# Small products and transposes in four column tiles: a two-layer attention and feed-forward kernel on one core

## The chip, the core and the metric

The kernel runs on one core of a Trainium2 chip. A core has five engines that work side by side and meet at semaphores: TensorE (matrix products, written to PSUM), VectorE, ScalarE, GpSimd, and SyncE, whose queue starts most transfers (SP in the profile). The metric is the device time of the program in microseconds; each kernel's time is the median of several runs. A profile is one execution taken by the hardware profiler; its span runs from the first to the last instruction.

TensorE computes `out = lhsT.T @ rhs`: a weight load puts `lhsT` into the array (PEld in the profile), a matmul streams `rhs` through it (PE). The array can be used in one piece, in four row tiles (four products with up to 32 rows of contraction each, side by side) or in four column tiles (four products with 32 output rows each, side by side). The profile shows this in the form: `128*128` is a whole product, `128*32` one of four column tiles, `32*128` or `16*128` a row tile.

## What is computed

Four layers alternate over x of 2048 x 512 in bf16: attention with a memory (A), feed-forward (B), A, B, each on a layer norm and added to x.

```
def A(x):   # 32 heads of 16, four segments of 512 rows
    q, k, v = heads(x @ wq), heads(x @ wk), heads(x @ wv)
    phi = lambda t: where(t > 0, t + 1, exp(t))
    M, z = 0, 0
    for s in range(4):
        a_dot = causal_softmax(q[s] @ k[s].T * scale) @ v[s]
        a_mem = (phi(q[s]) @ M) / (phi(q[s]) @ z + 1e-6)
        out[s] = g * a_mem + (1 - g) * a_dot
        M = M + phi(k[s]).T @ v[s]
        z = z + sum(phi(k[s]))
    return out @ wo
def B(x):
    return (gelu(x @ w_gate) * (x @ w_up)) @ w_down
```

In segment 0 the memory is empty, so the memory products run in segments 1 to 3, and the update of M in segments 0 to 2, in both attention layers.

## The kernel before

Everything lies in SBUF: x as 16 tiles of 128 x 512 (`x_sb`) and all weights. The two attention layers have four segments each, so that there are eight attention steps k = 0 to 7 (`Att`) and eight feed-forward steps (`Ffn`), one per segment and layer; step k of `Ffn` follows step k of `Att`, and step k + 4 of `Att` follows step k of `Ffn`. Work of several steps is interleaved.

The order of all instructions is made by a planner that runs in Python when the program is built. `Clocks` keeps an estimate of TensorE's time (`ck.pe`) and of each other engine's, with a cost for each operation; `Item` is a piece of TensorE work with a due time, a condition under which it is ready, its operations and what follows when they are done. The loop at the end of the kernel takes, in this order: a score step when a score buffer is free, the next operation of the opened item, a new item that is ready and has the earliest due time, or, when nothing of that is to be had and scores remain, one product of `warm` with itself whose result nobody reads. Each engine works through its instructions in the order so made; the planner's times decide that order only, and semaphores keep the data right.

TensorE's work, by the lines of the profile:

- Line 395, in `product`: all dense products (q, k, v, the output projection wo, gate, up, down), each 128 x 512 with a contraction of 128 per call, issued as four column tiles of 32 output rows. The unread products of `warm` in the loop are also made here.
- Line 800: scores, in row tiles, two heads to a score buffer `st` of two PSUM banks. ScalarE exponentiates them (line 829) into `pt`, GpSimd masks the diagonal blocks (line 820).
- Line 848: the flush, probabilities times v, in column tiles: 16 matmuls, four for each of four key blocks, with 512, 384, 256 and 128 columns. VectorE transposes the result back (line 860), divides and adds.
- Line 645, `den_mm`: phi(q) times z, 16 products of 128 x 8 for each attention step with a memory. Line 665, `num`: phi(q) times M, 16 products of 128 x 128 a step, four to an item. Line 716, `upd_item`: phi(k).T times v, 16 products of 128 x 128 a step, accumulated in one bank. All three are whole products.
- Line 486, `turn_item`: transposes of the normed rows `xn` into `xnT`. Most norms are transposed by a transfer on SP's queue (line 359). For three feed-forward steps, 0, 1 and 7 (`BY_PE`), TensorE does it, four 128 x 128 transposes for each of the four row tiles, as whole operations with a bf16 result in PSUM. Ahead of each four stand two unread whole products of 128 x 256 (line 484, `FILL = 2`), and the item counts as ready that much earlier. VectorE or ScalarE evicts the result (lines 385 and 386, in `evict`), whichever the planner finds free.

`ck.tiling(mode)` tells the planner's clock of a change of tiling and adds `SWITCH` to it; `whole(fn)` wraps an operation with `ck.tiling("whole")`. It emits nothing by itself. `ALWAYS = True` makes `product` take the column tiles in every case.

Of the kernel before, what the change touches and what calls it, by code (L numbers as in the profile page):

```python
# [14 lines left out]
BF16 = mybir.dt.bfloat16  # L15
I32 = mybir.dt.int32

P = 128
D = 512
H = 32  # L20
DH = 16
NSEG = 4
NK = 2 * NSEG
L = 512
NT = 16
KT = D // P
FF = 1792
FT = FF // P
TPS = L // P
# [20 lines left out]
EXP_SLACK, E_SLACK, PHI_SLACK, GELU_SLACK = -1.0, 3.0, 3.0, -1.0  # L50
ACT_EVICT, FIRST_EVICT = 0.5, 1.0
XN_BUFS = 3
FILL = 2
KB_DVE = 1
KB_SLACK = 4.0
HALF_STEPS = 1
MARGIN = 1.0
MEM_SLACK = 1.0
ALWAYS = True


class Engine:
# [157 lines left out]
def kernel(  # L220
# [14 lines left out]
    nc = tc.nc  # L235
# [9 lines left out]
    ck = Clocks()  # L245
# [30 lines left out]
    for n, (sb, w) in enumerate(((wg_sb, B_w_gate), (wu_sb, B_w_up))):  # L276
        for kt in range(KT):
            for h in range(2):
                c = slice(FF * h // 2, FF * (h + 1) // 2)
                pieces.append((37.0 + 1.6 * (8 * n + 2 * kt + h), 224, lambda sb=sb, w=w, kt=kt, c=c: load(  # L280
                    sb[:, kt, c], w_view(w)[:, kt, c])))
    for h in range(7):
        r = slice(2 * h, 2 * h + 2)
# [4 lines left out]
    warm = cst.tile([P, P], BF16, name="warm")  # L288
    wide = warm[:].unsqueeze(1).to_broadcast([P, 4, P])
    nc.vector.memset(warm[:], 1.0)  # L290

    def bank_tile(i, shape, dtype=F32):
        return psp.tile(shape, dtype, tag=f"m{i}", bufs=1, name="m")
# [11 lines left out]
    ident = cst.tile([P, P], BF16, name="ident")  # L305
# [21 lines left out]
    def by_head(va):  # L327
        return va[:, :, 0:VW].rearrange("p t (h e) -> p t h e", e=DH + 1)
# [24 lines left out]
    def turn_later(t, slack, out, in_, landed, margin=0.0):  # L353

        def told(t2):
            t3 = max(t2 + 1.4 + margin, ck.dma + 1.2)
            ck.at(t3 - 0.2, lambda: landed(t3))

        ck.sp.post(t, slack, (1.3, lambda: nc.sync.dma_start_transpose(out=out(), in_=in_()), told))
# [16 lines left out]
    def evict(ps, dst, src, told, slack=NORMAL):  # L376

        taken = []

        def end(t):  # L380
            ps.read(t)
            told(t)

        first = FIRST_EVICT if ("scores", HALF_STEPS - 1) not in ev and HALF_STEPS else ACT_EVICT
        ck.dve.post(ck.made(), slack, (0.673, lambda: nc.vector.tensor_copy(out=dst(), in_=src()), end), taken=taken)  # L385
        ck.act.post(ck.made(), slack + first, (0.602, lambda: nc.scalar.activation(  # L386
            out=dst(), in_=src(), func=ACT.Copy), end), taken=taken)

    def product(out, lhsT, rhs, start=True, stop=True):

        if ck.mode == "columns" or ALWAYS:
            ck.tiling("columns")
            for c in range(4):
                r = slice(32 * c, 32 * c + 32)
                nc.tensor.matmul(out[r], lhsT=lhsT[:, r], rhs=rhs, start=start, stop=stop, tile_position=(0, 32 * c))  # L395
        else:
            ck.tiling("whole")
            nc.tensor.matmul(out, lhsT=lhsT, rhs=rhs, start=start, stop=stop)

    def whole(fn):  # L400
        return lambda: (ck.tiling("whole"), fn())

    def dense(ps, pairs):
        n = len(pairs)
# [6 lines left out]
    class Norm:  # L411
# [64 lines left out]
        def turn_item(self, j, xn, t, landed):  # L476

            ps = Psum()
            half = L // 2

            def turned():
                return ps()[:, 0:half].bitcast(BF16).rearrange("p (k t) -> p k t", t=P)

            ops = [(Clocks.MM[512] / 2, whole(lambda: nc.tensor.matmul(
                ps()[:, half:L], lhsT=warm[:], rhs=wide[:, 0:2, :], start=True, stop=True)))] * FILL
            ops += [(Clocks.MM[128], whole(lambda kt=kt: nc.tensor.transpose(
                turned()[:, kt, :], xn()[:, kt * P:(kt + 1) * P], ident[:]))) for kt in range(KT)]
            return Item(-0.5, lambda: t + Engine.LATENCY <= ck.pe + FILL * Clocks.MM[512] / 2, ops,
                        lambda: evict(ps, lambda: self.xnT[:, :, j * P:(j + 1) * P], turned, landed, URGENT),
                        kind="turn", ps=ps)  # L490

# [11 lines left out]
    items = []  # L503
# [5 lines left out]
    class Att:  # L509
# [126 lines left out]
        def mem_items(self):  # L636
            k = self.k

            def ready(*more):
                return ck.has(*[("phiq", k, b) for b in range(4)], ("mem", k - 1), *more)  # L640

            den = Psum((P, TPS, 4, 8))

            def den_mm(j, b):
                nc.tensor.matmul(den()[:, j, b, :], lhsT=self.phiq[:, b, j * P:(j + 1) * P],  # L645
                                 rhs=mem_state[k - 1][1][:, b, :], start=True, stop=True)

            def den_done():
                def add():
                    self.rdm = wrk.tile([P, TPS, 4, 8], F32, tag="rdm", bufs=1, name="rdm")  # L650
                    nc.vector.tensor_scalar(out=self.rdm[:], in0=den()[:], scalar1=EPS_MEM, scalar2=None, op0=ALU.add)

                ck.dve.post(ck.made(), NORMAL, (0.273, add, den.read),
                            (0.956, lambda: nc.vector.reciprocal(out=self.rdm[:], in_=self.rdm[:]),
                             lambda t: ev.update({("den", k): t})))

            items.append(Item(k + 0.01, lambda: ready() and (self.s == 1 or ("am", k - 1) in ev),
                              [(Clocks.SMALL, whole(lambda j=j, b=b: den_mm(j, b))) for j in range(TPS) for b in range(4)],
                              den_done, kind="mem", ps=den))

            def num(b):
                ps = Psum()

                def mm(j):
                    nc.tensor.matmul(ps()[:, j * P:(j + 1) * P], lhsT=self.phiq[:, b, j * P:(j + 1) * P],  # L665
                                     rhs=mem_state[k - 1][0][:, b, :], start=True, stop=True)

                def done():
                    self.n_num += 1
                    if self.n_num == 4:  # L670
                        ev["memn", k] = ck.pe

                    def scale():
                        self.am = seg.tile([P, TPS, P], BF16, tag=f"am{b % 2}", bufs=1, name="am")
                        nc.vector.tensor_tensor(
                            out=self.am[:].rearrange("p t (h e) -> p t h e", e=DH),
                            in0=ps()[:].rearrange("p (t h e) -> p t h e", h=8, e=DH),
                            in1=self.rdm[:, :, b, :].unsqueeze(3).to_broadcast([P, TPS, 8, DH]),
                            op=ALU.mult)

                    def told(t):
                        ps.read(t)
                        am = self.am
                        self.n_am += 1
                        if self.n_am == 4:
                            ev["am", k] = t
                        self.amT[b] = seg.tile([P, L], BF16, tag=f"amT{b}", bufs=1, name="amT")
                        turn_later(t, NORMAL, lambda: self.amT[b][:].rearrange("p (t q) -> p t q", q=P),
                                   lambda: am[:].rearrange("p t d -> p (t d)"),
                                   lambda t2: ck.at(t2 + 1.0, lambda: ev.update({("amT", k, b): t2 + 1.0})))  # L690

                    ck.dve.post(ck.made(), NORMAL, (0.683, scale, told))

                def go():
                    return (ready(("den", k)) and (b < 2 or ("amT", k, b - 2) in ev)
                            and (self.s == 1 or (("amT", k - 1, (b + 2) % 4 if b < 2 else b) in ev
                                                 and ("aT", k - 1, b) in ev)))

                return Item(k + 0.02 + 0.001 * b, go, [(Clocks.MM[128], whole(lambda j=j: mm(j))) for j in range(TPS)], done,
                            kind="mem", ps=ps)  # L700

            for b in range(4):
                items.append(num(b))

        def upd_item(self):
            k = self.k
            psm = Psum((P, 4, P))
            n_mm = 4 * TPS
# [4 lines left out]

            def m(c):
                j, b = divmod(c, 4)
                nc.tensor.matmul(psm()[:, b, :], lhsT=self.phik[:, j, b * P:(b + 1) * P],  # L716
                                 rhs=by_head(self.vaug)[:, j, 8 * b:8 * b + 8, 0:DH], start=(c == 0), stop=(c == n_mm - 1))

            def done():
                ev["upd", k] = ck.pe  # L720
# [22 lines left out]
                else:  # L743
# [5 lines left out]
                             (0.2, z, told)]  # L749
                ck.dve.chain(ck.made(), MEM_SLACK, *steps)  # L750

            items.append(Item(k + 0.45, ready, [(Clocks.MM[128], whole(lambda c=c: m(c))) for c in range(n_mm)],
                              done, kind="upd", ps=psm))


# [250 lines left out]
    mem_state = {}  # L1006
# [40 lines left out]
    ps = bank_tile(1, [P, L])  # L1047
# [4 lines left out]
    ps, half = bank_tile(2, [P, L]), L // 2  # L1052
# [5 lines left out]
    ps = bank_tile(3, [P, L])  # L1058
# [24 lines left out]
    opened, half = None, 0  # L1083
# [49 lines left out]
    while streams or items or opened or ck.busy():  # L1133
# [3 lines left out]
        if halves:  # L1137
            half = score(halves)
            continue
        if opened:  # L1140
            cost, fn = opened.ops.pop(0)
# [14 lines left out]
        if halves:  # L1156
            half = score(halves)
            continue
        if min(banks) <= ck.pe:

            if streams:
                ps = Psum()
# [37 lines left out]
```

## Time and profile before

| | us |
|---|---|
| three runs, median | 567.98 |
| lowest and highest | 567.58, 568.27 |
| profiled execution, its span | 566.8 |
| ScalarE's exponentials of scores (line 829), busy | 310.6 |
| den products (line 645), busy | 3.8 |
| num products (line 665), busy | 8.1 |
| upd products (line 716), busy | 7.4 |
| transposes (line 486), busy | 4.6 |
| unread products ahead of them (line 484), busy | 5.0 |

A group's row reads: line, engine, operation, output<-inputs, form, count | busy time of the group, mean length of one in ns | idle time of the engine ahead of it, and who ended most of it. Matmul records overlap, since the next product starts while the one before runs out of the array: busy time and length of a record say less than the distance from one start to the next. A row of the timeline reads: start, length from the first start to the last end, engine, line, operation, tiles, form of the first, count of instructions merged.

### The profile page before, as it was taken

To read this page: it belongs to the slowest core of one execution; us is meant where nothing else is said; L and a number is where in the kernel's file an instruction comes from. 1 tells how busy PE (TensorE), PEld (TensorE's weight loads), DVE (VectorE), ACT (ScalarE), POOL (GpSimd) and SP (SyncE) were. 2 spreads that over 40 slices of the span, in tenths; PEclk is the share of its full clock that TensorE was granted. 3 is DMA by queue.
4 is the path that set the end of the run, shared out by engine and by line. 5 is a ranking of instruction groups with operands and counts; after the bars stand their busy time and mean duration, and the time that the engine had idled before them with its cause. 6 is when DMAs were issued, how large, how long until landed. Compare 5 with 4: busy or idle time off the path is not lost.

```text
span 566.8 us, 22572 instructions
## 1 busy us (share of the span) xinstructions
PE 557.4 (98%) x9966; PEld 259.0 (46%) x9966; DVE 460.5 (81%) x879; ACT 447.1 (79%) x512; POOL 271.1 (48%) x520
## 2 busy tenths in 40 slices
PE   8999999999999999999999999999999999999997
PEld 4433444444545444444444444444444444445554
DVE  5977989989999789878988989889688876787061
ACT  3899989988999779987889879988899776860600
POOL 2599854455542458435861557525664354310000
PEclk9999999999999999999999999999999999999999
DMA  7346613600330016200210124001320003100001
GB/s 223 41 104 196 132 20 41 159 13 16 44 60 1 3 39 78 31 12 2 54 26 3 30 43 72 12 3 30 87 39 3 3 12 86 21 2 30 12 3 39
DMA packets 64354, 25.85 MB, mean 46 GB/s; under 512 B 54272, under 2 KB 64256, under 8 KB 64256
## 3 DMA queue, kind: packets, MB, share of 16 engines
q1 hardware_dynamic: 64112, 24.40, 21.0%
q8 instruction: 78, 1.28, 1.0%
q14 instruction: 20, 0.16, 0.1%
q10 hardware_dynamic: 144, 0.01, 0.0%
HBM read 9.71 MB, written 2.10 MB: 21 GB/s over the span
## 4 chain that ended last, share of the span: by engine, by line
PE 86%; DVE 6%; ACT 5%; issue 2%; DMA 1%; POOL 0%; ACTq 0%
PE m L395 66%; PE st L800 9%; PE m L848 6%; ACT pt L829 2%; PE m L299 1%; PE m L716 1%; PE m L665 1%; ACT gel L1000 1%; DVE byq L860 1%; DMA phik<-e 1%; DVE aT L875 1%; DVE ab L868 1%; DVE st L424 0%; DVE q L385 0%; PE m L645 0%
## 5 line engine op out<-in xcount | busy, mean ns | idle before, releaser
L829 ACT ACTIVATE pt<-st 128x1024 bf16<-128x1024 f32 x320 | 310.6, 1028 | 55.5 <-PE st L800 48.4
L820 POOL TENSOR_SCALAR_AFFINE_SELECT pt<-pt 128x256 bf16<-128x256 bf16 (+1 forms) x448 | 204.9, 475 | 222.3 <-ACT pt L829 214.8
L395 PE MATMUL m<-xnT,wg_sb 128*32 128x512 bf16 x1792 | 108.3, 380 | 0.9 <-ACT xnT L386 0.7
L395 PE MATMUL m<-wd_sb,gel 128*32 128x512 bf16 x1792 | 105.6, 380 | 0.0
L395 PE MATMUL m<-xnT,wu_sb 128*32 128x512 bf16 x1792 | 102.8, 380 | 0.3 <-DVE vaug L385 0.3
L967 DVE TENSOR_TENSOR gel<-gel,m 128x512 bf16<-128x512 bf16 x112 | 74.4, 683 | 27.2 <-PE m L395 23.2
L395 PEld LDWEIGHTS <-wu_sb 128*32 128x32 bf16 x1792 | 47.9, 97 | 46.9 <-issue 4.5
L395 PEld LDWEIGHTS <-gel 128*32 128x32 bf16 x1792 | 46.0, 97 | 45.2 <-issue 5.1
L395 PEld LDWEIGHTS <-wg_sb 128*32 128x32 bf16 x1792 | 44.8, 96 | 46.0 <-issue 9.1
L914 DVE TENSOR_TENSOR x_sb<-x_sb,m 128x512 bf16<-128x512 bf16 x64 | 42.4, 675 | 23.3 <-PE m L395 23.0
L860 DVE STREAM_TRANSPOSE byq<-m 128x512 f32<-128x512 f32 x64 | 45.1, 706 | 14.3 <-PE m L848 13.9
L848 PE MATMUL m<-pt,vaug 128*32 128x512 bf16 (+3 forms) x1024 | 46.7, 301 | 0.1
L555 POOL TENSOR_SCALAR kB<-kf,maskB 128x512 bf16<-128x512 bf16 x28 | 44.4, 1586 | 4.4 <-DVE kf L385 3.1
L1000 ACT ACTIVATE gel<-gel 128x2048 bf16<-128x2048 bf16 (+1 forms) x28 | 45.2, 1685 | 0.1
L385 DVE CAST gel<-m 128x512 bf16<-128x512 f32 x56 | 37.8, 684 | 8.9 <-PE m L395 8.8
L424 DVE BATCH_NORM_STATS2 st<-x_sb 128x6 f32<-128x512 bf16 x60 | 40.7, 678 | 0.5
L800 PE MATMUL st<-q,kB 32*128 32x128 bf16 (+3 forms) x512 | 39.1, 300 | 0.8 <-ACT pt L829 0.7
L800 PE MATMUL st<-q,kf 16*128 16x384 bf16 (+3 forms) x512 | 39.1, 302 | 0.0
L848 PEld LDWEIGHTS <-vaug 128*32 128x32 bf16 x1024 | 25.3, 97 | 22.8 <-issue 2.8
L395 PE MATMUL m<-xnT,wq_sb 128*32 128x512 bf16 x496 | 33.9, 381 | 0.0
L395 PE MATMUL m<-xnT,wk_sb 128*32 128x512 bf16 x496 | 33.9, 381 | 0.0
L395 PE MATMUL m<-wo_sb,aT 128*32 128x512 bf16 x512 | 32.3, 380 | 0.9 <-DVE aT L878 0.8
(96 smaller groups left out, 563.7 us busy)
## 6 DMA issues: line engine op xcount, KB each, us to landing
out_dram<-x_sb SPq DMA_DIRECT2D x16, 128.0 KB, 1.7
wg_sb<-in_B_w_gate_dram SPq DMA_DIRECT2D x8, 224.0 KB, 4.7
wu_sb<-in_B_w_up_dram SPq DMA_DIRECT2D x8, 224.0 KB, 4.1
wd_sb<-in_B_w_down_dram SPq DMA_DIRECT2D x7, 256.0 KB, 4.9
x_sb<-in_A_x_dram SPq DMA_DIRECT2D x3, 512.0 KB, 6.1
xnT<-xn SPq DMA_TRANSPOSE x48, 2.6
x_sb<-in_A_x_dram SPq DMA_DIRECT2D x4, 128.0 KB, 2.8
wv_sb<-in_A_wv_dram SPq DMA_DIRECT2D x1, 512.0 KB, 7.0
```

What stands on the lines that cost most here:

```text
L385: ck.dve.post(ck.made(), slack, (0.673, lambda: nc.vector.tensor_copy(out=dst(), in_=src()), end), taken=taken)
L395: nc.tensor.matmul(out[r], lhsT=lhsT[:, r], rhs=rhs, start=start, stop=stop, tile_position=(0, 32 * c))
L424: nc.vector.bn_stats(out=self.st6[:, 0, :], in_=x_sb[:, self.tt0 + j, :])
L555: job.post(t, KB_SLACK if k else NORMAL, (cost, lambda: eng.tensor_scalar(out=self.kB[:, b, :], in0=self.kf[:, b, :], scalar1=maskB[:, 0:1 ...
L800: nc.tensor.matmul(sts[j // 2][:, j % 2, c0:c0 + N], lhsT=lhsT[rows, b, P * ki:P * ki + P], rhs=self.q[rows, b, P * ki:L], start=True, sto ...
L820: nc.gpsimd.affine_select(out=dv, in_=dv, pattern=[[0, w], [1, P]], compare_op=ALU.is_ge, fill=0.0, base=0, channel_multiplier=-1)
L829: ck.act.post(max(begun + 0.4, self.step_from), EXP_SLACK, (1.024, lambda st=st, pt=pt: nc.scalar.activation(out=pt[:], in_=st[:], func=AC ...
L848: nc.tensor.matmul(ps()[32 * j:32 * j + 32, P * ki:L], lhsT=self.vaug[:, ki, h * (DH + 1):h * (DH + 1) + 32], rhs=two[j // 2][:, j % 2, c0 ...
L860: nc.vector.transpose(out=self.byq[:, par, :, :].rearrange("p a c -> p (a c)"), in_=ps()[:])
L914: ck.dve.post(ck.made(), slack, (0.683, lambda: nc.vector.tensor_tensor(out=xt, in0=xt, in1=ps()[:], op=ALU.add), lambda t: (ps.read(t), t ...
L967: ck.dve.post(ck.made(), NORMAL, (0.683, lambda: nc.vector.tensor_tensor(out=g, in0=g, in1=ps()[:], op=ALU.mult), lambda t: (ps.read(t), e ...
L1000: return (0.205 + 0.427 * (f1 - f0), lambda: nc.scalar.activation(out=g, in_=g, func=ACT.Gelu_apprx_tanh), lambda t: ev.update({("gel", se ...
```

## The change

The memory products (den, num, upd) and the transposes of `turn_item` go through `product`, so that each is issued as four matmuls of 32 columns of weights in four column tiles. The transposes thereby become ordinary products with the identity, with an fp32 result that fills the whole PSUM bank instead of a bf16 result in its half; the evictions read fp32. The two unread products ahead of each four transposes go, and the item counts as ready when its xn is. `whole`, `FILL` and `ALWAYS` go. The planner's costs of the operations stay as they were per product. The four transposes of each row tile in the prologue (`first_turn`), and the prologue's products, stay whole.

```diff
-FILL = 2
-ALWAYS = True
@@ product
-        if ck.mode == "columns" or ALWAYS:
-            ck.tiling("columns")
-            for c in range(4):
-                r = slice(32 * c, 32 * c + 32)
-                nc.tensor.matmul(out[r], lhsT=lhsT[:, r], rhs=rhs, start=start, stop=stop, tile_position=(0, 32 * c))
-        else:
-            ck.tiling("whole")
-            nc.tensor.matmul(out, lhsT=lhsT, rhs=rhs, start=start, stop=stop)
-
-    def whole(fn):
-        return lambda: (ck.tiling("whole"), fn())
+        ck.tiling("columns")
+        for c in range(4):
+            r = slice(32 * c, 32 * c + 32)
+            nc.tensor.matmul(out[r], lhsT=lhsT[:, r], rhs=rhs, start=start, stop=stop, tile_position=(0, 32 * c))
@@ turn_item
-            half = L // 2
-                return ps()[:, 0:half].bitcast(BF16).rearrange("p (k t) -> p k t", t=P)
-            ops = [(Clocks.MM[512] / 2, whole(lambda: nc.tensor.matmul(
-                ps()[:, half:L], lhsT=warm[:], rhs=wide[:, 0:2, :], start=True, stop=True)))] * FILL
-            ops += [(Clocks.MM[128], whole(lambda kt=kt: nc.tensor.transpose(
-                turned()[:, kt, :], xn()[:, kt * P:(kt + 1) * P], ident[:]))) for kt in range(KT)]
-            return Item(-0.5, lambda: t + Engine.LATENCY <= ck.pe + FILL * Clocks.MM[512] / 2, ops,
+                return ps()[:].rearrange("p (k t) -> p k t", t=P)
+            ops = [(Clocks.MM[128], lambda kt=kt: product(turned()[:, kt, :], xn()[:, kt * P:(kt + 1) * P], ident[:]))
+                   for kt in range(KT)]
+            return Item(-0.5, lambda: t + Engine.LATENCY <= ck.pe, ops,
@@ mem_items
-                nc.tensor.matmul(den()[:, j, b, :], lhsT=self.phiq[:, b, j * P:(j + 1) * P],
-                                 rhs=mem_state[k - 1][1][:, b, :], start=True, stop=True)
+                product(den()[:, j, b, :], self.phiq[:, b, j * P:(j + 1) * P], mem_state[k - 1][1][:, b, :])
-                              [(Clocks.SMALL, whole(lambda j=j, b=b: den_mm(j, b))) for j in range(TPS) for b in range(4)],
+                              [(Clocks.SMALL, lambda j=j, b=b: den_mm(j, b)) for j in range(TPS) for b in range(4)],
-                    nc.tensor.matmul(ps()[:, j * P:(j + 1) * P], lhsT=self.phiq[:, b, j * P:(j + 1) * P],
-                                     rhs=mem_state[k - 1][0][:, b, :], start=True, stop=True)
+                    product(ps()[:, j * P:(j + 1) * P], self.phiq[:, b, j * P:(j + 1) * P], mem_state[k - 1][0][:, b, :])
-                return Item(k + 0.02 + 0.001 * b, go, [(Clocks.MM[128], whole(lambda j=j: mm(j))) for j in range(TPS)], done,
+                return Item(k + 0.02 + 0.001 * b, go, [(Clocks.MM[128], lambda j=j: mm(j)) for j in range(TPS)], done,
@@ upd_item
-                nc.tensor.matmul(psm()[:, b, :], lhsT=self.phik[:, j, b * P:(b + 1) * P],
-                                 rhs=by_head(self.vaug)[:, j, 8 * b:8 * b + 8, 0:DH], start=(c == 0), stop=(c == n_mm - 1))
+                product(psm()[:, b, :], self.phik[:, j, b * P:(b + 1) * P],
+                        by_head(self.vaug)[:, j, 8 * b:8 * b + 8, 0:DH], c == 0, c == n_mm - 1)
-            items.append(Item(k + 0.45, ready, [(Clocks.MM[128], whole(lambda c=c: m(c))) for c in range(n_mm)],
+            items.append(Item(k + 0.45, ready, [(Clocks.MM[128], lambda c=c: m(c)) for c in range(n_mm)],
```

The planner runs anew for the changed kernel, so that the order of all work behind the prologue can come out otherwise.

## The prediction

> **What bounds the kernel now.** I read the page first: busy shares of the engines, then the chain that ended last.
>
> ```profile
> span 566.8 us, 22572 instructions
> PE 557.4 (98%) x9966; PEld 259.0 (46%) x9966; DVE 460.5 (81%) x879; ACT 447.1 (79%) x512; POOL 271.1 (48%) x520
> PE 86%; DVE 6%; ACT 5%; issue 2%; DMA 1%; POOL 0%; ACTq 0%
> L829 ACT ACTIVATE pt<-st 128x1024 bf16<-128x1024 f32 x320 | 310.6, 1028 | 55.5 <-PE st L800 48.4
> ```
>
> TensorE is busy 98% of the span and holds 86% of the chain. The last row shows who waits for whom: ScalarE's exponentials, the largest work of another engine, stood idle 55.5 us, 48.4 of them for TensorE's scores. So a microsecond taken out of TensorE's stream is a microsecond off the end unless a new wait eats it. Next, the table by stage:
>
> ```profile
> 100.00:200.00 100.00, 99.27 (x1836) 47.42 (x1836) 90.51 (x176) 89.44 (x100) 46.29 (x92) 1.00 0.22 40
> 400.00:500.00 100.00, 99.66 (x1836) 45.89 (x1832) 77.92 (x136) 81.62 (x87) 46.50 (x93) 1.00 0.16 33
> 500.00:567.00 67.00, 62.00 (x1128) 33.37 (x1120) 31.84 (x54) 16.00 (x23) 2.79 (x6) 1.00 0.06 18
> ```
>
> The columns after the length are TensorE's matmuls, its weight loads, VectorE, ScalarE and GpSimd; then the granted clock, 1.00 throughout. In the middle TensorE is full, and no other engine is.
>
> But busy is not the same as productive: matmul records overlap. What one costs is the distance between starts. The timeline, cut to TensorE, shows it (start, length, rows merged):
>
> ```profile
> 86.60 0.40 PE L800 MATMUL st<-q,kf 16*128 16x512 bf16 x4
> 86.93 0.56 PE L645 MATMUL m<-zcols,phiq 128*128 128x8 bf16 x16
> 87.42 1.05 PE L395 MATMUL m<-xnT,wg_sb 128*32 128x512 bf16 x16
> 88.29 0.72 PE L848 MATMUL m<-pt,vaug 128*32 128x512 bf16 x16
> 88.83 0.61 PE L395 MATMUL m<-xnT,wg_sb 128*32 128x512 bf16 x8
> 89.37 0.40 PE L800 MATMUL st<-q,kf 16*128 16x384 bf16 x8
> 89.70 0.62 PE L395 MATMUL m<-xnT,wg_sb 128*32 128x512 bf16 x8
> 90.25 0.62 PE L665 MATMUL m<-mblk,phiq 128*128 128x128 bf16 x8
> 90.80 1.05 PE L395 MATMUL m<-xnT,wg_sb 128*32 128x512 bf16 x16
> ```
>
> Three tilings alternate: rows (L800), columns (128*32, L395 and L848), whole (128*128). The durations to take off the last instruction of a merged row:
>
> ```profile
> L395 PE MATMUL m<-xnT,wg_sb 128*32 128x512 bf16 x1792 | 108.3, 380 | 0.9 <-ACT xnT L386 0.7
> L848 PE MATMUL m<-pt,vaug 128*32 128x256 bf16 x256 | 18.2, 273 | 0.0
> L665 PE MATMUL m<-mblk,phiq 128*128 128x128 bf16 x96 | 8.1, 221 | 0.0
> L716 PE MATMUL m<-vaug,phik 128*128 128x128 bf16 x96 | 7.4, 224 | 1.1 <-DMA phik<-e 1.1
> L645 PE MATMUL m<-zcols,phiq 128*128 128x8 bf16 x96 | 3.8, 168 | 0.0
> L486 PE MATMUL m<-ident,xn 128*128 128x128 bf16 x48 | 4.6, 220 | 0.0
> ```
>
> Four groups of four (87.42, x16): (1.05-0.38)/3 = 0.22 us for four column tiles of 512; below, "a four" is one product in four column tiles. Whole products: L665 (0.62-0.22)/7 = 0.057 us each, L645 (0.56-0.17)/15 = 0.026.
>
> **What a change of tiling costs.** Rows to whole: 86.60 to 86.93 is 0.33 for a 512-wide set, 0.11 over its 0.22. Whole to columns: L645's last starts at 86.93+0.39 = 87.32, the next at 87.42: 0.10 against 0.026, so 0.07; L665's last starts at 90.65, the next at 90.80: 0.15 against 0.057, so 0.09. Columns to whole: two fours from 89.70 are through at 90.13 by their rate, the whole one starts at 90.25: 0.11. Columns to rows: 88.83 to 89.37 is 0.54 for two fours of 0.22, 0.10. All changes thus cost 0.07 to 0.11 us; I take 0.10, and 0.095 for those with a whole side.
>
> **The change, part by part.** Counts are read off the order in which the two built programs issue TensorE's work. Mode changes: 412 before (333 between rows and columns, 79 with a whole side), 360 after (359 and 1). It is not 79 fewer, since a memory product between two score steps now costs a change on either side as a column item. Removed 78 x 0.095 = 7.4 us, added 26 x 0.10 = 2.6: **-4.8 us**. They lie in TensorE's stream, on the path.
>
> The filling products go:
>
> ```profile
> 77.64 0.38 PE L484 MATMUL m<-warm 128*128 128x256 bf16 x2
> 77.86 0.39 PE L486 MATMUL m<-ident,xn 128*128 128x128 bf16 x4
> L484 PE MATMUL m<-warm 128*128 128x256 bf16 x24 | 5.0, 276 | 0.0
> L395 PE MATMUL m<-warm 128*32 128x512 bf16 x112 | 8.5, 384 | 0.1
> ```
>
> Two take 0.22 us, so 24 take **-2.6 us**. But the planner puts unread products (the last row: 112, so 28 fours) where it finds nothing to do while scores remain, and the new order has 160 of them, 40 fours: 12 x 0.22 = **+2.6 us**. Three of the 28 stand late, from the last block of scores on; of the 40, 14 do. That is work that runs out: a part of the gain turned back into waiting in the plan itself. The removal may also uncover a late xn, at most where each pair stood: 12 x 0.22 = 2.6 us, none if xn is there; that is part of the +0.6 below.
>
> Now the products themselves: 96 num, 96 upd and 48 transposes of 128 columns become 240 fours, 96 den products of 8 columns become 96 fours. Instructions rise from 9,966 to 10,998 matmuls. A 128-wide four occurs in the flushes only. The flush at 88.29 is four sets of 512, 384, 256 and 128 columns, and the next column product starts at 88.83: 0.54 us for 1,280 columns, where 0.217 per 512 (the 1.05-us row of 87.42 with 16, less its last record and a stagger of 0.01) gives 0.54. So its 128-wide four costs no more than its share, 0.056, as a whole product does: +0.0 for the 240. For the 8-wide four no row exists. From below it is the whole product's 0.026 (cost 0; not much less, since the starts inside a four already take 0.01: 0.61 at 88.83 is 0.22+0.38 and this 0.01, so at most 1.5 us would be gained), from above the 128-wide four's 0.056 (+0.03 x 96 = 2.9). The shape is nearer to the 8-wide whole product, so I take 0.031: **+0.5 us**. Both bounds presume that fours of this size can follow each other at that rate for 16 in a row, which no row shows; the second rival is that they can't.
>
> The Trainium skill speaks against the change here: its page "TensorEngine Tiling (Array Packing)", section "Restrictions", says that column tiling switches the fast weight load off, and "TensorE: Matmul & The Clock Gate", section "LDWEIGHTS (loading the stationary operand)", prices a load at its columns over 1.2 ns. My estimate from these: 27 ns a tile, 107 ns a four if its four loads follow each other, and the sum would be 96 x 81 + 240 x 51 ns, 20 us worse. The trace disagrees on the serial reading: the flush's 128-wide four at 0.056 us has four such loads for its successor under it.
>
> Evictions: the transposes were bf16 in PSUM, as products they are fp32.
>
> ```profile
> L385 DVE COPY xnT<-m 128x512 bf16<-128x512 bf16 x4 | 1.7, 424 | 2.3 <-PE m L486 2.3
> L385 DVE CAST gel<-m 128x512 bf16<-128x512 f32 x56 | 37.8, 684 | 8.9 <-PE m L395 8.8
> L386 ACT ACTIVATE xnT<-m 128x512 bf16<-128x512 bf16 x8 | 4.6, 606 | 20.3 <-PE m L486 20.3
> L386 ACT ACTIVATE gel<-m 128x512 bf16<-128x512 f32 x42 | 24.6, 613 | 2.6 <-PE m L395 2.4
> 527.02 1.69 PE L395 MATMUL m<-xnT,wg_sb 128*32 128x512 bf16 x28 [0.69 <-ACT xnT L386]
> ```
>
> On VectorE 684 instead of 424 ns, on ScalarE nothing. 3 of the 12 are in VectorE's order after (the first prologue's four stay as they are). 0.26 x 3 = 0.8 at most, and it is bare only where the gate products wait for it, as in the last row; elsewhere flushes and scores cover it. If that cover goes, gate products and the weight loads queued behind them wait. I take **+0.2**.
>
> Moved work: VectorE gets 2 evictions more, ScalarE 2 fewer (the planner's choice); SP's queue issues the same transfers, with one phik transpose moved ahead of three loads of wd_sb early on. The transposes serve updates later than that and wd_sb serves down products later still; both queues have slack, cost 0. What they would cost uncovered: a late phik is the wait of 1.1 us in L716's row, so that is the bound. For waits that come to lie otherwise in the new order I take **+0.6**; the bounds are -1.1 (L716's wait gone) and about +4, the idle time that the last stage has in all besides its store (67.0-62.0 = 5.0 less the final eviction of 0.7).
>
> Sum: -4.8-2.6+2.6+0.5+0.2+0.6 = -3.5. Against the profiled span 566.8 that is 563.3; the runs' median, 567.98, lies 1.2 above the span. Forecast: 568.0-3.5 = **564.5 us**.
>
> **The rivals.**
>
> *The saved time stays on TensorE as waiting* (same). Scores need ScalarE's exponentials to free st; if these set the pace wherever a change is saved, only the tail gains. For it: 14 late unread fours instead of 3, and VectorE and ScalarE near 90% in the middle. Against: ScalarE's 48.4 us of waiting for TensorE. In this case the 4.8 are refilled: 567 to 568.
>
> *Small fours are bound by instructions* (slower). One mechanism: if each small product needs the 0.026 us that L645's whole products take from start to start, whatever its tile, a four needs 0.10. Price: 96 x (0.104-0.026) + 240 x (0.104-0.057) = 7.5+11.3 = 18.8 us, at the memory items and transposes, 568.0-4.0+18.8 = 583 us with the other terms. It decides from a mean of 4.8/336 = 14 ns per four on. If work queued ahead carries part of each burst, 570 to 575. For it: bursts of 16 fours are 128 instructions, more than stand in any row here at that density. Against: 16 matmuls of a flush with as many loads went by in about half a microsecond, 0.03 each, and the four of a set start within 0.01. The Trainium skill, "TensorE: Matmul & The Clock Gate", section "Wait — 56ns, not 53.3ns?", states such a floor of about 25 ns however small the product; "The mechanism" on the same page has tiles 4 ns apart. The trace agrees with both and cannot show which rules an 8-wide four.
>
> *The new order collides* (slower). The planner's choices all move; one gate stage that waits for a late xnT or a mask costs about 1 us (0.69 above), four of them more than the saving: 569.
>
> *The edit does nothing*: excluded by the order, 52 changes fewer.
>
> **How the numbers follow.** Forecast 0.62, refilled 0.15, instruction-bound 0.13, collision 0.10. A measurement of this kernel tells 0.2%, 1.1 us, from no change. The likeliest case alone spans 561.0 (all fours free, 1.1 us of wait gone, no +0.6) to 567 (den at its upper bound). The range takes in the refilled case, the collision and the mild form of the instruction bound: 561.0 to 572; left out is the full 583 and a better luck than the bounds. Faster: 0.62 plus some of the refilled case, 0.64; same 0.12; slower 0.24.
>
> **What would show it.** In the changed profile: no 128*128 rows behind the prologue; den rows (128*32, 128x8) 16 fours in about 0.5 us plus a record, not 1.6; num and upd fours 0.056 apart, not 0.10; item to item without the 0.1 steps; VectorE's xnT eviction at 684 ns. I am wrong if the den or upd bursts stretch, if gate products wait more than 1 us for xnT, or if scores wait for ScalarE by several microseconds in all.

## The result, and the profile after

The changed kernel takes 564.75 us (median of four runs, 564.4 to 565.5) against 567.78 for the kernel before beside it: a ratio of 0.9947, 95% interval 0.9932 to 0.9961, so 3.0 us faster. The forecast was 564.5. The profiled execution spans 563.2 us (forecast 563.3).

First the page of the kernel after: span, engines, the chain by engine, and ScalarE's exponentials.

```profile
span 563.2 us, 24630 instructions
PE 553.9 (98%) x10998; PEld 259.7 (46%) x10998; DVE 464.7 (83%) x881; ACT 446.8 (79%) x510; POOL 273.1 (48%) x520
PE 82%; DVE 15%; issue 1%; DMA 1%; POOL 0%; ACT 0%; DVEq 0%
L815 ACT ACTIVATE pt<-st 128x1024 bf16<-128x1024 f32 x320 | 310.4, 1027 | 56.4 <-PE st L786 52.6
```

TensorE is as full as before, and ScalarE still waits for its scores, 52.6 us now. VectorE has moved from 6% to 15% of the chain: the chain follows one of several nearly equal paths, and no wait of TensorE's as long as that stands behind it.

The timeline of the changed kernel, TensorE alone, over the stretch that the prediction read (start, length, line, tiles, form of the first, how many merged):

```profile
85.03 0.33 PE L392 MATMUL m<-zcols,phiq 128*32 128x8 bf16 x28
85.29 0.40 PE L786 MATMUL st<-q,kf 16*128 16x512 bf16 x4
85.62 0.41 PE L392 MATMUL m<-zcols,phiq 128*32 128x8 bf16 x36
85.86 1.92 PE L392 MATMUL m<-xnT,wg_sb 128*32 128x512 bf16 x32
87.59 0.73 PE L834 MATMUL m<-pt,vaug 128*32 128x512 bf16 x16
88.14 0.24 PE L392 MATMUL m<-mblk,phiq 128*32 128x128 bf16 x4
88.31 0.40 PE L786 MATMUL st<-q,kf 16*128 16x384 bf16 x8
88.64 0.57 PE L392 MATMUL m<-mblk,phiq 128*32 128x128 bf16 x28
89.04 1.90 PE L392 MATMUL m<-xnT,wg_sb 128*32 128x512 bf16 x32
90.87 0.29 PE L786 MATMUL st<-q,kf 16*128 16x256 bf16 x4
```

The steps from a memory item to a dense product are gone. Nine den fours start at 85.62, and the gate product follows at 85.86: 0.24 us, 0.027 a four and no 0.07 behind it. Seven num fours go from 88.64 to 89.04, 0.40 us or 0.057 each, where the whole products needed another 0.09. What is left are the changes to and from the row tiles of the scores: 0.33 us from 85.29 to 85.62 for a set of 0.22.

The groups of the changed kernel by form, small products and unread ones:

```profile
L392 PE MATMUL m<-warm 128*32 128x512 bf16 x160 | 11.7, 383 | 0.1
L392 PE MATMUL m<-mblk,phiq 128*32 128x128 bf16 x384 | 8.5, 219 | 0.0
L392 PE MATMUL m<-vaug,phik 128*32 128x128 bf16 x384 | 7.1, 223 | 0.0
L392 PE MATMUL m<-ident,xn 128*32 128x128 bf16 x192 | 4.3, 220 | 0.6 <-DVE x_sb L900 0.4 <-DVE xnT L383 0.2
L392 PE MATMUL m<-zcols,phiq 128*32 128x8 bf16 x384 | 4.2, 170 | 0.0
```

Four times as many records, and nearly the same busy time: 8.5 against 8.1, 7.1 against 7.4, 4.3 against 4.6, 4.2 against 3.8 us. The transposes show a wait that was not there, 0.6 us. The timeline of the changed kernel at that place, TensorE first, then VectorE:

```profile
142.47 0.41 PE L392 MATMUL m<-ident,xn 128*32 128x128 bf16 x16
143.28 0.41 PE L392 MATMUL m<-ident,xn 128*32 128x128 bf16 x16 [0.41 <-DVE x_sb L900]
143.88 0.41 PE L392 MATMUL m<-ident,xn 128*32 128x128 bf16 x16 [0.19 <-DVE xnT L383]
144.22 0.39 PE L786 MATMUL st<-q,kB 32*128 32x512 bf16 x2
144.54 0.64 PE L392 MATMUL m<-zcols,phiq 128*32 128x8 bf16 x64
145.02 0.62 PE L392 MATMUL m<-wv_sb,xnT 128*32 128x512 bf16 x8
```

```profile
141.33 1.31 DVE L445 TENSOR_SCALAR xn<-x_sb,mv,rs 128x512 bf16<-128x512 bf16 x3
142.56 0.67 DVE L900 TENSOR_TENSOR x_sb<-x_sb,m 128x512 bf16<-128x512 bf16 x1
143.15 0.68 DVE L383 CAST xnT<-m 128x512 bf16<-128x512 f32 x1
```

Four fours take 0.23 us; here 0.81 and 0.60 lie between the starts, 0.96 us lost. The rows it waited for were not late: VectorE had made three xn by 142.64. The second and the third set start 0.05 us after L900 and L383 end (143.23 and 143.83), and both of these read a result m out of PSUM. In the trace it is the product, which writes PSUM, that waits for VectorE, and not the weight load, which reads xn. So the wait is most likely for a PSUM bank that VectorE had still to read, at a place where pairs of unread products stood before. The den row shows the best measure of the 8-wide four: 16 in 0.48 us, 0.030 each.

### The profile page after: what moved, and what is told of

It reads as the page before. It is cut to its first block, busy times and chain, and to the rows that moved or that the text cites. A ratio compares the mean times of both kernels' runs of the same rounds, so it can differ in the third digit from the quotient of the medians.

```text
span 563.2 us, 24630 instructions
## 1 busy us (share of the span) xinstructions
PE 553.9 (98%) x10998; PEld 259.7 (46%) x10998; DVE 464.7 (83%) x881; ACT 446.8 (79%) x510; POOL 273.1 (48%) x520
## 4 chain that ended last, share of the span: by engine, by line
PE 82%; DVE 15%; issue 1%; DMA 1%; POOL 0%; ACT 0%; DVEq 0%
PE m L392 66%; PE st L786 8%; PE m L834 5%; DVE st L415 2%; DVE x_sb L900 2%; DVE byq L846 1%; PE m L297 1%; DVE e L604 1%; DVE phiq L604 1%; DVE e L618 1%; DVE xn L445 1%; DVE aT L861 1%; DVE gel L383 1%; DMA amT<-am 1%; DVE ab L854 1%
## 5 line engine op out<-in xcount | busy, mean ns | idle before, releaser
L815 ACT ACTIVATE pt<-st 128x1024 bf16<-128x1024 f32 x320 | 310.4, 1027 | 56.4 <-PE st L786 52.6
L392 PE MATMUL m<-xnT,wu_sb 128*32 128x512 bf16 x1792 | 104.1, 379 | 0.0
L392 PEld LDWEIGHTS <-wg_sb 128*32 128x32 bf16 x1792 | 45.5, 96 | 46.0 <-issue 10.3
L900 DVE TENSOR_TENSOR x_sb<-x_sb,m 128x512 bf16<-128x512 bf16 x64 | 42.5, 675 | 22.0 <-PE m L392 21.6
L383 DVE CAST gel<-m 128x512 bf16<-128x512 f32 x56 | 37.9, 683 | 10.7 <-PE m L392 10.3
L786 PE MATMUL st<-q,kf 16*128 16x128 bf16 (+3 forms) x512 | 39.5, 302 | 0.7 <-ACT pt L815 0.7
L392 PE MATMUL m<-wv_sb,xnT 128*32 128x512 bf16 x512 | 32.3, 380 | 0.0
```

Of the source, the lines that this page charges most:

```text
L786: nc.tensor.matmul(sts[j // 2][:, j % 2, c0:c0 + N], lhsT=lhsT[rows, b, P * ki:P * ki + P], rhs=self.q[rows, b, P * ki:L], start=True, sto ...
L815: ck.act.post(max(begun + 0.4, self.step_from), EXP_SLACK, (1.024, lambda st=st, pt=pt: nc.scalar.activation(out=pt[:], in_=st[:], func=AC ...
L900: ck.dve.post(ck.made(), slack, (0.683, lambda: nc.vector.tensor_tensor(out=xt, in0=xt, in1=ps()[:], op=ALU.add), lambda t: (ps.read(t), t ...
```

## Where the time is: one account for all kernels

For each pair of neighbouring steps I took the distance between the starts of TensorE's products from the trace and compared it with what that step takes when nothing is in the way: 216, 162, 109, 56 and 25 ns for 512 to 8 columns, plus 93 to 106 ns at a change of tiling. What is over by more than 40 ns is a wait; the prologue's first 12 us are left out. Unread work is 0.216 us a four and 0.109 a 256-wide product. Some records are missing, so a sum is good to about 1 us.

| kernel | median | span | tiling changes | unread, us | waits, us | both |
|---|---|---|---|---|---|---|
| before | 567.8 | 566.8 | 412 | 8.7 | 6.2 | 14.9 |
| changed | 564.75 | 563.2 | 360 | 8.6 | 7.0 | 15.6 |
| e1, order of before, column tiles | 566.0 | 564.5 | 362 | 8.7 | 8.0 | 16.7 |
| e2, order of after, whole | 568.4 | 566.8 | 418 | 8.6 | 5.6 | 14.2 |
| e3, memory products only | 571.6 | 569.5 | 368 | 9.1 | 12.1 | 21.2 |
| e4, transposes only | 571.1 | 569.3 | 409 | 6.9 | 10.2 | 17.1 |
| e5, unread products removed only | 570.0 | 568.0 | 426 | 6.3 | 8.5 | 14.8 |
| e6, den twice | 575.1 | 573.9 | 360 | 8.6 | 14.3 | 22.9 |
| e7, whole products put in | 570.1 | 568.3 | 405 | 8.6 | 7.4 | 16.0 |
| e8, no unread fours | 570.8 | 568.8 | 362 | 0 | 20.0 | 20.0 |
| p1, before, second plan | 571.55 | 569.7 | 421 | 8.2 | 7.3 | 15.5 |
| p1, changed, second plan | 565.75 | 564.8 | 370 | 5.2 | 10.3 | 15.5 |
| p2, before, third plan | 570.9 | 568.4 | 420 | 9.3 | 7.0 | 16.3 |
| p2, changed, third plan | 567.8 | 565.5 | 368 | 5.8 | 11.2 | 17.0 |

The last column is the main find. The less unread work a plan has, the more it waits, as a rule; the sum stays between 14.2 and 17.1 us in 11 of the 14 (e1, e2, e6 and e7 repeat the plan of one of the two kernels, so these are ten plans in all). Two of the others hold something else: about 1.4 us of e6's waits and 4.6 of e8's lie where TensorE's clock was granted at half, and 5.4 of e6's are the four gaps described below. Without these the sums are 16.1 and 15.4. Only e3 stays outside, with 9.1 us unread and 12.1 of waits, and that is not explained. So unread products are, in the main, idle time under another name here.

## The experiments

### The order held, the tiling changed, and the reverse

e1 keeps the plan of the kernel before and issues its small products in column tiles; e2 keeps the plan of the changed kernel and issues them whole. In both, VectorE, ScalarE and GpSimd run the same operations in the same order as their parent.

```diff
 e1, on the kernel before: a helper that tells the planner nothing
+    def fours(out, lhsT, rhs, start=True, stop=True):
+        for c in range(4):
+            r = slice(32 * c, 32 * c + 32)
+            nc.tensor.matmul(out[r], lhsT=lhsT[:, r], rhs=rhs, start=start, stop=stop, tile_position=(0, 32 * c))
...
-                nc.tensor.matmul(den()[:, j, b, :], lhsT=self.phiq[:, b, j * P:(j + 1) * P],
-                                 rhs=mem_state[k - 1][1][:, b, :], start=True, stop=True)
+                fours(den()[:, j, b, :], self.phiq[:, b, j * P:(j + 1) * P], mem_state[k - 1][1][:, b, :])
 e2, on the changed kernel, for den, num, upd and the transposes
+    def one(out, lhsT, rhs, start=True, stop=True):
+        ck.tiling("columns")
+        nc.tensor.matmul(out, lhsT=lhsT, rhs=rhs, start=start, stop=stop)
```

> The order of the kernel before on every engine, but memory products, transposes and the unread products ahead of them issued in column tiles. Tiling changes in TensorE's order fall from 412 to 362, unread work stays. My theory (the gain is the changes of tiling, 0.1 us each): 567.8-5.0+0.5 for the 8-wide fours = 563.3 us. Rival 'the new order is what gains': 567.8. Rival 'the unread products ahead of the transposes gain it': 567.8.

> The order of the changed kernel on every engine, but memory products and transposes (as products with an fp32 result) issued whole. Tiling changes rise from 360 to 418. My theory: 564.75+58 x 0.1-0.5 = 570.0 us, slower than the kernel before, since its order spends 12 more unread fours and gains only through the tiling. Rival 'the new order is what gains': 564.7.

Measured: e1 565.98 us, a ratio of 0.9966 (0.9954 to 0.9977) to the kernel before; e2 568.41, 1.0011 (1.0002 to 1.0020). In one and the same order the tiling is worth 1.8 us in the plan of before (567.74 to 565.98) and 3.7 in the new one (568.41 to 564.75). So the order alone gains nothing: left whole, it is 0.7 slower. Neither value is the 4.5 to 5.3 that the expectations had. The account shows most of the reason: 50 and 58 changes fewer are there, about 5 and 5.7 us, but waits grow by 1.8 and 1.4 us, presumably as TensorE gets ahead of the others. With 0.5 us for the 8-wide fours that leaves 2.7 and 3.8 us; the first closes only to the account's 1 us.

### One part alone, planned anew

e3 puts only the memory products through `product` and keeps the transposes; e4 is the change in `turn_item` alone; e5 sets `FILL = 0` in the kernel before.

```diff
 e3, on the kernel before (num and upd alike); turn_item as it was
+                product(den()[:, j, b, :], self.phiq[:, b, j * P:(j + 1) * P], mem_state[k - 1][1][:, b, :])
...
-                              [(Clocks.SMALL, whole(lambda j=j, b=b: den_mm(j, b))) for j in range(TPS) for b in range(4)],
+                              [(Clocks.SMALL, lambda j=j, b=b: den_mm(j, b)) for j in range(TPS) for b in range(4)],
 e5, on the kernel before
-FILL = 2
+FILL = 0
```

> Only the memory products in column tiles; transposes whole, with their unread products; planned anew. 368 tiling changes against 412 (-4.4), 2 unread fours more (+0.4), 8-wide fours +0.5. My theory: 567.8-3.5 = 564.3 us, nearly all of the change's gain. Rival 'the unread products ahead of the transposes gain it': 567.8 us.

> Only the transposes changed: in column tiles, and no unread products ahead of them; memory products whole; planned anew. 409 tiling changes against 412, 24 unread 256-wide products fewer (-2.6), 4 unread fours more (+0.9). My theory: 567.8-0.3-2.6+0.9+0.2 = 566.0 us. Rival 'the unread products ahead of the transposes gain it': 564.8 us.

> The kernel before without the unread products ahead of the transposes, everything whole as before; planned anew. 426 tiling changes against 412 (+1.4), 24 unread products fewer (-2.6), one unread four more (+0.2). My theory: 567.8-1.0 = 566.8 us. Rival 'the unread products ahead of the transposes gain it': 564.8 us.

Measured: 571.57 (1.0069, 1.0057 to 1.0082), 571.08 (1.0057, 1.0041 to 1.0072) and 570.01 us (1.0045, 1.0028 to 1.0061). All three expectations failed, and so did the rival: every part alone is slower than no part. The counts of tiling changes came out as stated, 368, 409 and 426; what was not in the sums are waits. The largest in e3 and in e4 follow, from their timelines, and then the longest idle time of e5 that is new (a longer one, 0.90 us at 144.32, has its like in the kernel before, 0.73 us at 143.60):

```profile
342.90 0.83 PE L395 MATMUL m<-xnT,wg_sb 128*32 128x512 bf16 x12 [1.53 <-DMA xnT<-xn]
```

```profile
413.39 1.05 PE L395 MATMUL m<-xnT,wg_sb 128*32 128x512 bf16 x16 [0.88 <-DMA xnT<-xn]
```

```profile
223.98 0.40 PE L395 MATMUL m<-xnT,wg_sb 128*32 128x512 bf16 x4 [0.84 <-DVE am L675]
```

Gate products stand at the head of TensorE's queue and wait for a transpose by transfer, or for VectorE. By the order that it made, the planner had taken these for done. That is the rival "the new order collides", at places that differ from plan to plan. In e5 the account closes with it: 14 changes more cost 1.4 us, unread and waits together are the same, and the span is 1.2 longer. (The medians differ by 2.3, so that about 1 us stays open.) Taking out 2.6 us of unread work gained nothing.

### Prices by themselves

e6 issues each den four twice. e7 puts one whole product of 8 columns ahead of each num item, where the num products then overwrite it.

```diff
 e6
+                for _ in range(2):
                     product(den()[:, j, b, :], self.phiq[:, b, j * P:(j + 1) * P], mem_state[k - 1][1][:, b, :])
 e7
                 def mm(j):
+                    if j == 0:
+                        nc.tensor.matmul(ps()[:, 0:8], lhsT=self.phiq[:, b, 0:P],
+                                         rhs=mem_state[k - 1][1][:, b, :], start=True, stop=True)
                     product(ps()[:, j * P:(j + 1) * P], self.phiq[:, b, j * P:(j + 1) * P], mem_state[k - 1][0][:, b, :])
```

> The price of a change of tiling by itself: the changed kernel with one whole 8-wide product ahead of each of the 24 num items (its result is overwritten); order otherwise unchanged. 405 tiling changes against 360, and 24 whole products of 0.026. My theory, 0.07 to 0.11 a change: 564.75+45 x 0.09+0.6 = 569.4 us. Rival 'changes of tiling are hidden in a real stream': 564.75+0.6 = 565.4 us.

Measured: 570.08 us, 5.3 above the changed kernel. Less 24 x 0.026 that is 4.7 us for 45 changes, 0.105 each. Both times have intervals of about 0.8 us to either side, which is 0.03 a change, and 0.4 us of the 4.7 stands as added waits in the account, which would leave 0.096. Either way the price holds in a full stream. In e7's timeline one such product stands between column tiles:

```profile
88.04 0.73 PE L837 MATMUL m<-pt,vaug 128*32 128x512 bf16 x16
88.71 0.18 PE L653 MATMUL m<-zcols,phiq 128*128 128x8 bf16 x1
88.82 0.24 PE L392 MATMUL m<-mblk,phiq 128*32 128x128 bf16 x4
```

The flush's 0.54 us are over at 88.58, the whole product starts at 88.71 and the next at 88.82: 0.13 and 0.11.

> The changed kernel with each of the 96 den fours issued twice (the second overwrites the first with the same values), order otherwise unchanged. My theory, an 8-wide four costs 0.031 us: 564.75+96 x 0.031 = 567.7 us. Rival 'bound by instructions', 0.10 us a four: 564.75+10.0 = 574.7 us; each burst of 32 fours then shows 3.3 us instead of 1.0.

Measured: 575.1 us (1.0134, 1.0113 to 1.0156). The total is the rival's number, and the rival is wrong all the same. From e6's timeline, TensorE's rows of two bursts, the second cut at its start by the view:

```profile
146.26 1.11 PE L392 MATMUL m<-zcols,phiq 128*32 128x8 bf16 x120
149.11 0.21 PE L392 MATMUL m<-zcols,phiq 128*32 128x8 bf16 x8 [1.74 <-issue]
149.16 0.84 PE L392 MATMUL m<-wv_sb,xnT 128*32 128x512 bf16 x8
...
321.33 0.45 PE L392 MATMUL m<-zcols,phiq 128*32 128x8 bf16 x34
321.80 0.59 PE L392 MATMUL m<-xnT,wq_sb 128*32 128x512 bf16 x5
323.68 0.83 PE L392 MATMUL m<-xnT,wq_sb 128*32 128x512 bf16 x11 [1.28 <-issue]
```

30 fours ran in (1.11-0.17)/30 = 0.031 us each; a floor of 0.10 would have made 3 us of the first row. Then TensorE stood still for 1.9 us with nothing that the profile shows to wait for. The same happened ahead of 88.67, 323.68 and 482.72; from start to start, less the steps themselves, the four gaps cost 5.4 us. After the one that ended at 149.11 the clock was down, after the others it was not. From e6's table by stage (length, TensorE's busy time and count, weight loads, VectorE, ScalarE, GpSimd, clock, DMA):

```profile
147.20:149.10 1.90, 0.17 (x21) 0.09 (x11) 1.90 (x4) 1.18 (x2) 0.99 (x2) 1.00 0.00 0
150.00:151.00 1.00, 1.00 (x10) 0.30 (x14) 0.65 (x1) 0.00 (x0) 0.00 (x0) 0.50 0.07 16
153.00:154.00 1.00, 1.00 (x18) 0.26 (x17) 0.96 (x2) 1.00 (x2) 0.41 (x1) 1.00 0.00 0
```

The clock was granted at half from 149.4 to 152.8, and products of 0.216 took 0.43. So the 10.3 us are 96 x 0.031 = 3.0, four gaps 5.4, and the slow clock 1.7 at most, half of its 3.4 us.

What the gaps seem to wait for stands in the records of the queue that the page calls q8 instruction. In e6 it moves 89 packets of 16 KB, in the kernel before 78. TensorE has 22,764 and 19,932 products and weight loads in the two, so that a packet comes to 256 of them in both, at 64 bytes each:

```
gap ends at us   with product   packet landed at us   gap ends after it
 88.67           1500           n = 10,  87.31        1.36
149.11           2780           n = 20, 147.70        1.41
323.68           6359           n = 48, 322.15        1.53
482.72           9684           n = 74, 481.32        1.40
```

Each gap ends 1.4 to 1.5 us after a packet has landed, at product 128 n + 212 to 220, and a packet mostly starts near product 128 n + 98. Some 120 products with their loads lie between the two; when they go by in less than the 1 us of the packet and these 1.4, TensorE would have no instructions. 32 fours are 128 products in a microsecond. All four gaps fit this, but no run changed the fetching itself, so the cause is argued and not shown. In the changed kernel the nearest case leaves 1.73 us between landing and need (product 128 n + 212), at 88.9, and no gap shows; in the kernel before it was never under 4.2. In two other plans of the changed kernel (p1 and p2, below) the nearest cases leave 1.43 and 1.31 us, at 213.3 and 212.2, still with no gap over 0.1 us. So, by this reading, the change has used up a reserve that it did not know of.

### Without the unread fours

```diff
-                product(ps()[:], warm[:], wide)
```

> The changed kernel without the 40 unread fours of the planner's loop (8.6 us of TensorE work at most); order otherwise unchanged, nothing else left out. They stand where the planner found nothing ready, so most of them cover a wait that stays. My theory: part of them is late by the planner's clock only, a quarter of 8.6 comes off: 562.6 us. Rival 'the saved time stays on TensorE as waiting': 564.7 us, the waits stand in place of the fours.

Measured: 570.8 us, a ratio of 1.0057 (1.0045 to 1.0069) to the kernel before and 6 us slower than the changed kernel, which neither expectation had. This is no test in a fixed order: the removed call had also told the planner's clock of a tiling change, and the plan came out new (500 operations on ScalarE instead of 510). An order held fixed without the fours was not tried. What it does show, in the stretch from 70 to 80 us, first e8, then the changed kernel:

```profile
70.00:80.00 10.00, 7.45 (x164) 3.46 (x156) 9.74 (x22) 9.05 (x11) 6.30 (x14) 0.80 0.10 21
```

```profile
70.00:80.00 10.00, 9.59 (x242) 4.92 (x238) 9.76 (x23) 9.51 (x13) 5.88 (x13) 1.00 0.24 28
```

TensorE waits in place of the fours, and over this stretch its clock is granted at 0.80: it stood idle for 1.04 us ahead of 73.42 and 1.07 us ahead of 75.86, and from 75.9 to 82.8 the clock was at half. So in this plan idle time cost more than itself. That the unread fours protect the clock in the changed kernel is a guess from this, not shown.

### Two more plans of the same pair

By now the luck of a plan had moved kernels by 3 us, as much as the change. So both kernels were planned twice more, with a planner's price set differently: a tiling change at 0.104 instead of 0.097 us (p1), a 128-wide product at 0.060 instead of 0.056 (p2).

```diff
-    SWITCH = 0.097
+    SWITCH = 0.104
...
-    MM = {512: 0.2158, 128: 0.056}
+    MM = {512: 0.2158, 128: 0.060}
```

> Two further plans of the same pair, to tell the change from the luck of one plan. Here the kernel before with the planner's cost of a tiling change set from 0.097 to 0.104 us: the same work in another order. By steps: 421 tiling changes against 412 (+0.9), 26 unread fours against 28 (-0.4): 568.3 us; the waits that the order happens to make add or take up to 4 us (waits over 40 ns summed to 5.6 to 14.3 us in the eight kernels above that keep the unread fours).

> The changed kernel with the planner's cost of a tiling change at 0.104 us. 370 tiling changes against 360 (+1.0), 24 unread fours against 40 (-3.5): 562.3 us by steps, waits aside. Theory (the tiling gains 5 us of TensorE steps whatever the plan): 3 us or more below its partner. Rival 'the 3 us were the luck of one plan': no nearer to one side than plans of one kernel stand from each other.

> The kernel before with the planner's cost of a 128-wide product at 0.060 instead of 0.056 us. 420 tiling changes (+0.8), 31 unread fours (+0.6): 569.2 us by steps, waits aside.

> The changed kernel with the planner's cost of a 128-wide product at 0.060 us. 368 tiling changes (+0.8), 27 unread fours (-2.8): 562.8 us by steps, waits aside. Theory: 3 us or more below its partner; rival 'luck of one plan': no gap.

Measured: 571.55 and 565.75 us (p1), 570.89 and 567.81 (p2). The gaps of the pairs are -3.0 (the two original kernels), -5.8 and -3.1; the plans of one kernel stand 3.8 (before) and 3.1 us (changed) apart. In each pair the changed kernel is faster by 3 us or more, as expected. But the two plans of a pair have only the planner's price in common, and the changed kernel's third plan, 567.81, is no faster than the kernel before as given, 567.78. So a single plan of either is good to some 3 us only, and that the tiling gains something rests on e1 and e2, where the order is held. The times by steps of the changed kernel, 562.3 and 562.8, were missed by 3.5 and 5.0: the steps counted 16 and 13 unread fours fewer as gain, and waits took their place. Those of the kernel before, 568.3 and 569.2, were missed by 3.3 and 1.7. No plan beat the changed kernel as given.

## Why the prediction was right

**Tiling changes, -4.8 us: right as work taken off TensorE.** 52 fewer, as counted; e7 gives 0.096 to 0.105 each in the stream, hence -5.0 to -5.5, and the account -5.1 with each change at its own price. This is the cause of the gain: e2 takes it away in the changed kernel's own order and loses 3.7 us. Not all of it reaches the end, since waits grow with it: 1.8 us are left in e1 and 3.7 in e2.

**Unread products, -2.6 and +2.6: the sum right, the reading half right.** Both counts held. But they are not a gain and a loss of TensorE work: e5 and the last column of the account show that unread work and waits replace each other. The prediction said this of the 12 new fours ("waiting in the plan itself") and not of the 24 removed products, to which it gave a full 2.6; the only wait that it named behind their removal was a late xn. The waits that came at the transposes, 0.96 us, stand there with the xn made. The rival "the saved time stays as waiting" was thus true of this part.

**Small fours, +0.5: right.** 0.030 to 0.031 us for 8 columns against 0.031 forecast, 0.056 to 0.057 for 128. The Trainium skill, "TensorEngine Tiling (Array Packing)", section "Restrictions", says that column tiling switches the fast weight load off. Four loads one behind the other, which the prediction estimated from the skill at 0.107 us a four, did not show: 16 fours in a row took 0.030 each. The rival of a floor of 0.10 falls with e6's rows. Its weaker form, that long bursts outrun their instructions, came true only at twice the length, and, as it seems, by another mechanism.

**Evictions, +0.2.** From the groups of the changed kernel and its last norm:

```profile
L383 DVE CAST xnT<-m 128x512 bf16<-128x512 f32 x3 | 2.0, 680 | 0.0
L384 ACT ACTIVATE xnT<-m 128x512 bf16<-128x512 f32 x9 | 5.1, 601 | 17.8 <-PE m L392 17.6
523.44 0.83 PE L392 MATMUL m<-xnT,wg_sb 128*32 128x512 bf16 x12 [0.70 <-ACT xnT L384]
```

Three on VectorE at 680 ns (forecast 684), ScalarE as before, and the last gate waits 0.70 us as it did 0.69. One of VectorE's three ends TensorE's wait of 0.19 us at 143.88, about the 0.2 forecast, but at a transpose and not at a gate product; no wait of TensorE's names the other two.

**Waits of the new order, +0.6: the number lucky, the upper bound a little low.** Waits rose by 0.8 us. The late phik's 1.1 us went (0.0 idle in the upd products' row), and others of 1.9 us came, 0.96 of them at the transposes. But the other two plans of the changed kernel have 10.3 and 11.2 us of waits instead of 7.0, 4.1 and 5.0 above the kernel before, at and past the prediction's upper bound of about 4. That the forecast hit to 0.25 us is the luck of this plan.

**The unread late fours** stand where they were counted, in the changed kernel's timeline:

```profile
487.66 1.48 PE L392 MATMUL m<-xnT,wg_sb 128*32 128x512 bf16 x24
488.97 0.61 PE L392 MATMUL m<-warm 128*32 128x512 bf16 x8
489.51 0.39 PE L786 MATMUL st<-q,kB 32*128 32x512 bf16 x2
489.82 0.61 PE L392 MATMUL m<-warm 128*32 128x512 bf16 x8
490.37 0.39 PE L786 MATMUL st<-q,kB 32*128 32x512 bf16 x2
490.69 1.26 PE L392 MATMUL m<-warm 128*32 128x512 bf16 x20
491.78 0.72 PE L834 MATMUL m<-pt,vaug 128*32 128x512 bf16 x16
492.32 0.60 PE L392 MATMUL m<-warm 128*32 128x512 bf16 x8
```

Between the last gate product and the first up product 11 of the 14 fours, 2.4 us, fill a gap in which only scores and one flush run; the other three stand at 470 to 472 us. That gap is the next thing to attack.

**Open** is which of the planner's dates are wrong, so that its plans collide, why e3 has so much of both unread work and waits, and what sets the limit that e6 ran into and the other plans of the changed kernel came near.

## What to carry to other kernels

Count the changes of tiling in the issued order and price them from the distance of starts, about 0.1 us each here: small products are worth splitting into four column tiles when their neighbours are in columns, since at 8 and 128 columns the four cost no more than a few nanoseconds over the whole product. They are four times the instructions, though: bursts of 32 such fours were followed by gaps here. Add unread filler work to the waits before calling its removal a gain. Where a planner makes the order, a change of 3 us is shown by holding the order, as in e1 and e2, and not by one plan of each side, and a part tested alone by replanning tests the plan as much as the part.

## What the runs showed of the hardware

In e6 TensorE stood still four times, 0.6 to 1.9 us longer than its steps take, in or shortly behind a burst of 128 products with their loads in a microsecond, and each time until some 1.4 us after a 16 KB packet of its instruction queue had landed. That such bursts outrun the fetching of TensorE's own instructions fits all four gaps; no run tested it.

The clock was granted at half for 3.4 us after 1.74 us of idle time at 147.4 in e6. In e8 it was at half for 6.8 us after two idle stretches of 1.04 and 1.07 us (72.4 and 74.8), and for 3.4 us after three of 0.52 us between 25.7 and 28.1. Single idle stretches of 1.53 us in e3 (341.4) and 1.56 us in the changed kernel of p1 (495.8) left it at 1.00. So the length of one gap alone does not decide it in these runs.
